# Clears on GpSimd moved behind the x copies, first x tiles loaded from two queues, and some priorities of the instruction planner shifted, in a fused attention and token-mixing kernel

## The chip, the cores and the metric

The kernel runs on one core of one Trainium2 chip. The metric is the device time of one execution in microseconds (us). A profiled execution also has a span, from the first to the last instruction; here it is about 1.8 us shorter than the time. PE is TensorE's matmul unit, DVE is VectorE, ACT is ScalarE, POOL is GpSimd and SP is SyncE, which issues most of the DMA transfers.

Runs of this kernel fall into groups. Below, a "long run" is one more than 1.2 us above the fastest run of the same kernel, and the others are "short runs". Both kinds count as fast runs in the ratios, since the slow state begins at 1.5% above the fastest run; two long runs lie beyond that and are left out of the ratios (188.61 of before and 186.18 of short_close).

## The reference, cut to what matters

```python
x = A_x                                            # (1, 2048, 448) bf16
g = sigmoid((x * gate_w).sum(-1))
# A: 4 segments of 512 tokens, 16 heads of 28: causal softmax inside a segment,
#    plus a linear-attention memory of the segments before, mixed by sigmoid(beta), then @ wo
# B: h = layernorm(x); u = gelu(einsum('bsd,sf->bdf', h, w1) + b1)   # over tokens
#    y = einsum('bdf,fs->bds', u, w2) + b2, transposed back
return g * A(x) + (1 - g) * B(x)
```

## The kernel before

The program is a list of operations with the data they read and write. A planner simulates the five engines and takes, on each engine, the ready operation of the lowest priority number; each engine's instructions are then emitted in that order with semaphores. So a priority or a cost decides the final order.

The loads at the start (SP issues twelve, ACT five):

```python
load_x("SP", 0, 2)                       # x tiles 0 and 1, 224 KB
load_w(wk_nat, WK, R_wk, "wk", P_wk)     # SP: rows 0-255, rows 256-383; ACT: the last 64 rows
load_x("SP", 2, 2)
load_w(wq_nat, WQ, R_wq, "wq", P_wq)     # SP, and the last 64 rows from ACT
load_w(lambda: wvx, WV, R_wv, "wv")      # the same
op("ACT", ... gstage[0:3, :] ...)        # gate weights, two small loads
op("ACT", ... gstage[3:4, :] ...)
# [cut] x tiles 4-15 on SP, beta and the biases
```

The clears on POOL, free to start at once:

```python
op("POOL", lambda e: e.memset(vaug...[:, :, DH:32], 0.0), writes=R_v, name="v0", ...)
op("POOL", lambda e: e.memset(vaug...[:, :, DH : DH + 1], 1.0), reads=R_v, writes=R_v, name="v1", ...)
op("POOL", lambda e: e.memset(wo_sb[:], 0.0), writes=R_wo, name="wo0", ..., rel=8000.0)
op("POOL", lambda e: e.memset(maskg[:], 0.0), writes=[R_maskg], name="maskg0", ..., rel=8000.0)
```

The spread of WK into padded form on DVE, in three pieces as they arrive, which PE's first K projection needs:

```python
for k, (c0, c1) in enumerate(((0, 2), (2, 3), (3, 4))):
    op("DVE", lambda e, c0=c0, c1=c1: e.tensor_copy(wk_pad...[:, c0:c1, :, 0:DH]..., wk_nat()[:, c0:c1, :]...),
       reads=[R_wk[k]] + ..., writes=[R_wkp[k]], name=f"padk{k}", ...)
```

The end: every engine's list is emitted, and SP then waits until each output has landed.

```python
sch.plan()
totals = sch.finalize()
# [cut]
def emit(e, eng=eng):
    sch.emit_engine(e, eng, sems)
    if eng == "SP":
        for sp2 in sorted(sch.out_spaces):      # 17 outputs
            e.wait_ge(sems[sp2], totals[sp2])
```

## Time and profile before

| | before |
|---|---|
| three runs known at the prediction | 185.57, 186.44, 187.23 us (median 186.44) |
| span of the profiled run | 183.5 us (its time: 185.29) |
| PE busy | 96% of the span |
| PE's first K projection | 6.89 us |
| last output operation on DVE starts | 181.01 us |

The first projection and the last DVE operation cut the span into three parts: a start that waits for data (6.89), a long stretch in which PE is the bound (174.12), and a close of 2.5 us. The prediction shows the lines of the first two parts. It does not look at the close.

### The profile page before, as it was taken

How to read it: one execution, taken by the hardware profiler on the slowest of the kernel's cores; microseconds unless marked ns; L12 is line 12 of the kernel's file. 1: busy time of each engine (PE TensorE's matmuls, PEld its weight loads, DVE VectorE, ACT ScalarE, POOL GpSimd, SP SyncE). 2: the span in 40 equal slices, each digit the busy share in tenths (PEclk: the TensorE clock that was granted, in tenths of full speed). 3: DMA queues.
4: the chain of work that ended last, by engine and by line, in shares of the span. 5: the costliest groups of instructions: out<-in, count | busy, mean ns of one | idle time of the engine just before them, and what ended most of it. 6: DMA issues, size and time to landing. Idle time of an engine off the chain costs nothing.

```text
span 183.5 us, 3421 instructions
## 1 busy us (share of the span) xinstructions
PE 176.2 (96%) x1335; PEld 84.3 (46%) x1349; DVE 156.1 (85%) x307; ACT 130.9 (71%) x162; POOL 75.6 (41%) x108
## 2 busy tenths in 40 slices
PE   8599998999999999999999998999999999999994
PEld 3464433444445444444444453545445444445563
DVE  3799999879799999769898999998999989977122
ACT  1497879779999999998989997501799787600500
POOL 8500197143641715446292734512228537552000
PEclk9999999999999999999999999999999999999999
DMA  6998999005958271001446560276601702753001
GB/s 158 317 293 238 276 168 263 21 0 166 224 131 216 41 202 30 0 4 30 126 103 188 50 194 4 54 211 161 189 11 30 212 4 60 215 175 103 27 25 50
DMA packets 46427, 22.80 MB, mean 124 GB/s; under 512 B 11980, under 2 KB 46412, under 8 KB 46412
## 3 DMA queue, kind: packets, MB, share of 16 engines
q1 hardware_dynamic: 46164, 22.42, 48.2%
q8 instruction: 10, 0.16, 0.4%
q10 hardware_dynamic: 248, 0.17, 0.4%
q14 instruction: 5, 0.04, 0.1%
HBM read 18.13 MB, written 1.84 MB: 109 GB/s over the span
## 4 chain that ended last, share of the span: by engine, by line
PE 79%; DVE 10%; ACT 4%; POOL 3%; DMA 2%; issue 1%
PE t L950 24%; PE t L978 23%; PE t L634 10%; PE t L843 6%; PE t L880 6%; PE t L930 5%; PE t L691 3%; ACT t L852 2%; DMA t<-in_A_wk_dram 2%; PE t L726 2%; POOL t L798 2%; DVE t L567 1%; DVE t L788 1%; DVE t L804 1%; DVE t L940 1%; DVE t L704 1%
## 5 line engine op out<-in xcount | busy, mean ns | idle before, releaser
L852 ACT ACTIVATE t<-t 128x2048 bf16<-128x2048 f32 x40 | 75.3, 1883 | 9.8 <-PE t L843 9.7
L855 POOL TENSOR_SCALAR_AFFINE_SELECT t<-t 128x512 bf16<-128x512 bf16 x64 | 49.2, 769 | 52.6 <-ACT t L852 45.6
L950 PE MATMUL t<-t 128*128 128x448 bf16 x224 | 46.4, 353 | 0.3
L978 PE MATMUL t<-t 128*128 128x448 bf16 (+1 forms) x238 | 45.6, 342 | 0.2
L634 PE MATMUL t<-t 128*128 128x512 bf16 (+1 forms) x138 | 29.6, 355 | 2.2 <-DVE t L567 1.9
L978 PEld LDWEIGHTS t<-t 128*128 128x128 bf16 x238 | 22.4, 98 | 19.5 <-issue 1.8
L950 PEld LDWEIGHTS t<-t 128*128 128x128 bf16 x224 | 20.4, 98 | 21.5 <-issue 3.3
L910 POOL TENSOR_TENSOR t<-t 128x448 bf16<-128x448 f32 x12 | 15.3, 1272 | 24.4 <-DVE t L908 23.9
L634 PEld LDWEIGHTS t<-t 128*128 128x128 bf16 x144 | 13.3, 98 | 14.9 <-DVE t L567 2.4
L983 DVE SCALAR_TENSOR_TENSOR t<-t 128x448 bf16<-128x448 f32 (+1 forms) x17 | 11.1, 650 | 10.3 <-PE t L978 8.2
L843 PE MATMUL t<-t 28*128 28x512 bf16 (+3 forms) x256 | 15.8, 301 | 0.7 <-ACT t L705 0.4
L936 ACT ACTIVATE t<-t 128x448 bf16<-128x448 f32 x8 | 5.8, 725 | 11.9 <-PE t L930 11.7
L930 PE MATMUL t<-t 128*128 128x448 bf16 x64 | 13.8, 353 | 0.1
L691 PE MATMUL t<-t 128*128 128x449 bf16 x64 | 13.6, 353 | 0.0
L654 ACT ACTIVATE t<-t 128x512 bf16<-128x512 bf16 x12 | 7.5, 629 | 8.1 <-DMA t<-t 8.1
L896 DVE STREAM_TRANSPOSE t<-t 128x512 f32<-128x512 f32 x16 | 11.3, 704 | 1.6 <-PE t L880 1.5
L647 ACT ACTIVATE t<-t 128x512 bf16<-128x512 f32 (+1 forms) x16 | 8.1, 516 | 6.2 <-PE t L634 5.9
L916 DVE STREAM_TRANSPOSE t<-t 128x512 bf16<-128x512 bf16 x16 | 11.2, 699 | 0.7 <-POOL t L910 0.7
L880 PE MATMUL t<-t 128*32 128x512 bf16 (+3 forms) x256 | 11.6, 302 | 0.0
L967 DVE SCALAR_TENSOR_TENSOR t<-t 128x448 bf16<-128x448 f32 x14 | 10.7, 777 | 0.6 <-ACT t L965 0.5
L962 DVE SCALAR_TENSOR_TENSOR t<-t 128x448 f32<-128x448 f32 x14 | 9.7, 702 | 1.2 <-ACT t L957 1.1
L843 PEld LDWEIGHTS t<-t 28*128 28x128 bf16 x256 | 4.5, 92 | 13.1 <-ACT t L852 6.7
(89 smaller groups left out, 213.1 us busy)
## 6 DMA issues: line engine op xcount, KB each, us to landing
t<-in_B_w_dram SPq DMA_DIRECT2D x7, 1024.0 KB, 6.3
t<-in_B_w_dram SPq DMA_DIRECT2D x8, 896.0 KB, 5.2
out_dram<-t SPq DMA_DIRECT2D x15, 112.0 KB, 2.4
t<-in_A_x_dram SPq DMA_DIRECT2D x3, 448.0 KB, 6.7
t<-in_A_x_dram SPq DMA_DIRECT2D x2, 224.0 KB, 3.8
t<-in_A_wo_dram SPq DMA_DIRECT2D x4, 98.0 KB
t<-in_A_wq_dram SPq DMA_DIRECT2D x1, 336.0 KB, 4.9
t<-in_A_wv_dram SPq DMA_DIRECT2D x1, 336.0 KB, 5.2
```

The costliest lines, as they stand in the source:

```text
L634: last = e.matmul(bank(b)[:, 0:n], w_pad[0:CK, c, hg * 128 : hg * 128 + 128], xT[0:CK, c, tc * 512 + t0 : tc * 512 + t0 + n], start=(c == ...
L691: last = e.matmul(bank(b)[:, 0 : D + 1], xT[0:CK, c, t * 128 : t * 128 + 128], wvx[0:CK, c, 0 : D + 1], start=(c == 0), stop=(c == NCT - 1 ...
L843: last = e.matmul(bank(hl)[:, c0 : c0 + w], kT[r, hg, s * 512 + j * 128 : s * 512 + j * 128 + 128], qT[r, hg, s * 512 + 128 * j : s * 512 ...
L852: op("ACT", lambda e: e.activation(pslot(g), ps[:, 0:4, :], ACT.Exp, scale=SCALE), reads=R_bank[0:4], writes=[g.res], take=g, name=f"exp{p ...
L855: op("POOL", lambda e, c0=c0: e.affine_select(pslot(g)[:, :, c0 : c0 + 128], pslot(g)[:, :, c0 : c0 + 128], pattern=[[0, 4], [1, 128]], co ...
L880: last = e.matmul(bank(cb)[32 * hl : 32 * hl + 32, 128 * j : 512], vaug[:, 4 * s + j, 32 * h : 32 * h + 32], pslot(P_fill[u // 2][f])[:, h ...
L896: dv(lambda e: e.transpose(t2[:, 0, :], bank(cb)[:, 0:512]), [bres(cb)], [R_tt[tb][0]], "ta", 630, use=(cb,))
L910: op("POOL", lambda e: e.tensor_tensor(o3, n3[0], n3[1], op=ALU.add), reads=R_tt[tb], writes=[R_ob[tb]], name=f"o{u}", cost=1280, port=Tru ...
L916: dv(lambda e: e.transpose(oT[:, hg, s * 512 : s * 512 + 512], o), [R_ob[tb]], [R_qT[hg][s]], "ot", 635)
L930: last = e.matmul(bank(b)[:, 0:D], oT[:, hg, T * 128 : T * 128 + 128], wo_sb[:, hg, :], start=(hg == 0), stop=(hg == NHG - 1), skip_group_ ...
L950: op("PE", lambda e, st=st: e.matmul(bank(b)[:, 0:D], w1c[:, st, f2 * 128 : f2 * 128 + 128], xh[:, st, :], start=(st == 0), stop=(st == NT ...
L978: op("PE", lambda e, ft=ft: e.matmul(bank(b)[:, 0 : c1 - c0], w2c[:, ft, t2_ * 128 : t2_ * 128 + 128], uT[:, ft, c0:c1], start=(ft == 0), ...
```

## The change

The intent: POOL should not hold DVE up while DVE prepares the first projection (a copy of 448 columns took 1.47 us beside a clear and 0.26 later); the first x tiles should come from two queues; ACT should issue fewer loads (its five issues lasted until 3.65 us) and be free sooner; and a search with the planner gave 16 groups of operations other priorities. `COLD` is the planner's own estimate, in ns, of how long PE runs slowly at the start (by the clock record of the traces until 4.0 us before and 6.2 after), and it was changed too.

```diff
-COLD = 5000.0
+COLD = 3200.0
@@ plan
+        for o in self.ops:
+            o.prio = (o.prio[0] + shifts.get(o.name.split("-")[0], 0.0), o.idx)
+SHIFTS = (
+    ("mq3_3", -41.28), ("phk2_1", 0.29), ("phq2_2", 1.15), ("prk0_0", 0.51), ("prk0_1", 3.71), ("prk2_1", 10.16),
+    ("prk2_3", -7.78), ("prq2_3", -0.46), ("prt14", -56.47), ("prt3", 39.99), ("prt8", 6.09), ("prt9", -12.18),
+    ("pv0", 6.49), ("pv5", 23.25), ("sc2_1", -46.8), ("tm8", -43.02),
+)
@@ loads
-        op("ACT", lambda e: e.dma_start(dst()[64:128, 3, 0:D], src[384:448]), ...
+        op("SP" if take is not P_wk else "ACT", lambda e: e.dma_start(dst()[64:128, 3, 0:D], src[384:448]), ...
-    load_x("SP", 0, 2)
+    load_x("SP", 0, 1)
+    load_x("ACT", 1, 1)
-    op("ACT", lambda e: e.dma_start(gstage[0:3, :], ...
+    op("SP", lambda e: e.dma_start(gstage[0:3, :], ...
-    op("ACT", lambda e: e.dma_start(gstage[3:4, :], ...
+    op("SP", lambda e: e.dma_start(gstage[3:4, :], ...
@@ clears, now emitted after the x transposes
-    op("POOL", ... vaug ... 0.0), writes=R_v, name="v0", ...)
+        op("POOL", ... vaug ... 0.0), reads=[R_xT0[1][0]], writes=R_v, name="v0", ...)
-    op("POOL", ... wo_sb[:], 0.0), writes=R_wo, name="wo0", ..., rel=8000.0)
+        op("POOL", ... wo_sb[:], 0.0), reads=[R_xT0[1][0]], writes=R_wo, name="wo0", ...)
[the same for maskg0; renamed groups and one cost for the planner cut]
-    sch.plan()
+    sch.plan(SHIFTS)
```

`R_xT0[1][0]` is the second transposed block of x that DVE copies.

More of the change, by code (lines that the diff above doesn't have):

```diff
@@ L147, in op, with plan @@
         return o
-    def plan(self):
+    def plan(self, shifts=()):
         import bisect
+        shifts = dict(shifts)
+        for o in self.ops:
+            o.prio = (o.prio[0] + shifts.get(o.name.split("-")[0], 0.0), o.idx)
         succ = [[] for _ in self.ops]
@@ L450, in load_x @@
         op(eng, lambda e: e.dma_start(xh[:, t0 : t0 + n, :], xv[:, t0 : t0 + n, :]),
-           writes=R_x[t0 : t0 + n], name=f"ldx{t0}", dma=True, cost=500 if n == 2 else 1300, nbytes=n * 128 * 896)
+           writes=R_x[t0 : t0 + n], name=f"ldx{t0}", dma=True, cost=500 if n < 4 else 1300, nbytes=n * 128 * 896)
     def load_w(dst, src, r, name, take=None):
@@ L458, in load_w @@
                take=None if k else take)
-        op("ACT", lambda e: e.dma_start(dst()[64:128, 3, 0:D], src[384:448]), writes=[r[-1]], name="ld" + name + "b",
+        op("SP" if take is not P_wk else "ACT", lambda e: e.dma_start(dst()[64:128, 3, 0:D], src[384:448]),
+           writes=[r[-1]], name="ld" + name + "b",
            dma=True, cost=500, nbytes=57344)
@@ L472, in build_kernel @@
     load_w(lambda: wvx, WV, R_wv, "wv")
-    op("ACT", lambda e: e.dma_start(gstage[0:3, :], GW[0:384].rearrange("(c p) -> c p", p=128)),
+    op("SP", lambda e: e.dma_start(gstage[0:3, :], GW[0:384].rearrange("(c p) -> c p", p=128)),
        writes=[R_gst[0]], name="ldgw", dma=True, cost=500, nbytes=2000)
-    op("ACT", lambda e: e.dma_start(gstage[3:4, :], GW[320:448].rearrange("(c p) -> c p", p=128)),
+    op("SP", lambda e: e.dma_start(gstage[3:4, :], GW[320:448].rearrange("(c p) -> c p", p=128)),
        writes=[R_gst[1]], name="ldgwb", dma=True, cost=500, nbytes=2000)
@@ L529, in build_kernel @@
        name="wqp0", cost=pool_cost(256))
-    op("POOL", lambda e: e.memset(vaug.rearrange("p t (h c) -> p (t h) c", c=32)[:, :, DH:32], 0.0), writes=R_v,
-       name="v0", cost=pool_cost(1024))
-    op("POOL", lambda e: e.memset(vaug.rearrange("p t (h c) -> p (t h) c", c=32)[:, :, DH : DH + 1], 1.0),
-       reads=R_v, writes=R_v, name="v1", cost=pool_cost(256))
-    op("POOL", lambda e: e.memset(wo_sb[:], 0.0), writes=R_wo, name="wo0", cost=pool_cost(1792), rel=8000.0)
-    op("POOL", lambda e: e.memset(mhalf[:], -0.5), writes=[R_mhalf], name="mhalf", cost=200)
-    op("POOL", lambda e: e.memset(maskg[:], 0.0), writes=[R_maskg], name="maskg0", cost=pool_cost(512), rel=8000.0)
     def load_wo():
@@ L542, in load_wo, with pool_clears @@
                reads=[R_wv[0]], writes=[R_wo[hl]], name=f"ldwo{hl}", dma=True, cost=500, nbytes=126000)
+    def pool_clears():
+        op("POOL", lambda e: e.memset(vaug.rearrange("p t (h c) -> p (t h) c", c=32)[:, :, DH:32], 0.0),
+           reads=[R_xT0[1][0]], writes=R_v,
+           name="v0", cost=pool_cost(1024))
+        op("POOL", lambda e: e.memset(vaug.rearrange("p t (h c) -> p (t h) c", c=32)[:, :, DH : DH + 1], 1.0),
+           reads=R_v, writes=R_v, name="v1", cost=pool_cost(256))
+        op("POOL", lambda e: e.memset(wo_sb[:], 0.0), reads=[R_xT0[1][0]], writes=R_wo, name="wo0", cost=pool_cost(1792))
+        op("POOL", lambda e: e.memset(mhalf[:], -0.5), writes=[R_mhalf], name="mhalf", cost=200)
+        op("POOL", lambda e: e.memset(maskg[:], 0.0), reads=[R_xT0[1][0]], writes=[R_maskg], name="maskg0", cost=pool_cost(512))
     rr = [0]
@@ L628, in transposes_1, with proj_d @@
                alt=("ACT", lambda e, io=io: e.activation(*io(), ACT.Copy), act_cost(1024)))
-    def proj_d(w_pad, R_w, hg, tc, b, t0=0, n=512):
+    def proj_d(name, w_pad, R_w, hg, tc, b, t0=0, n=512):
         def fn(e):
@@ L639, in proj_d @@
         need = R_xT[tc] if tc else [r for h in range(2) if t0 < 256 * h + 256 and t0 + n > 256 * h for r in R_xT0[h]]
-        op("PE", fn, reads=need + R_w, writes=[bres(b)], **btake(b), name=f"prd{tc}_{hg}", mode="f",
+        op("PE", fn, reads=need + R_w, writes=[bres(b)], **btake(b), name=f"{name}{tc}_{hg}" + ("h" if t0 else ""), mode="f",
            cost=pe_cost(n, n, n, n), prio=PRJ[tc] + (0.01 if t0 else 0))
@@ L645, in do_k @@
         ks = kT[:, hg, tc * 512 + t0 : tc * 512 + t0 + n]
-        proj_d(wk_pad, R_wkp, hg, tc, b, t0, n)
+        proj_d("prk", wk_pad, R_wkp, hg, tc, b, t0, n)
         op("ACT", lambda e: e.activation(ks, bank(b)[:, 0:n], ACT.Copy),
@@ L667, in do_q @@
         qs = qT[:, hg, tc * 512 : tc * 512 + 512]
-        proj_d(wq_pad, R_wqp, hg, tc, b)
+        proj_d("prq", wq_pad, R_wqp, hg, tc, b)
         op("DVE", lambda e: e.tensor_copy(qs, bank(b)[:, 0:512]), **buse(b), reads=[bres(b)], writes=[R_qT[hg][tc]],
@@ L951, in mm1 @@
                                                start=(st == 0), stop=(st == NT - 1), skip_group_check=True),
-               reads=[R_slot[fb % NSL], R_x[st]], writes=[bres(b)], take=b if st == 0 else None, name=f"u{ft}_{st}", mode="f", cost=pe_cost(448),
+               reads=[R_slot[fb % NSL], R_x[st]], writes=[bres(b)], take=b if st == 0 else None, name=f"u{ft}-{st}", mode="f", cost=pe_cost(448),
                prio=P_M1 + ft)
@@ L981, in mm2 @@
                reads=[R_slot[r]] + (R_uT if ft == 0 else [R_uT[ft]]), writes=[bres(b)],
-               take=b if ft == 0 else None, name=f"y{T}_{ft}", mode="f", cost=pe_cost(c1 - c0), prio=P_M2 + T)
+               take=b if ft == 0 else None, name=f"y{T}-{ft}", mode="f", cost=pe_cost(c1 - c0), prio=P_M2 + T)
         op("DVE", lambda e: e.scalar_tensor_tensor(outst[:, p, c0:c1], bank(b)[:, 0 : c1 - c0], omg[:, T : T + 1],
@@ L996, in build_kernel @@
     transposes_0(1)
+    pool_clears()
     for t0 in (0, 256):
```

## The prediction

> **What bounds the kernel now.** I read the page first (engines, then the slices), then the chain that ended last, then the timeline of PE, DVE and POOL over the first 35 us, then the DMA issues. From the page, PE's row and two groups:
>
> ```profile
> PE 176.2 (96%) x1335; PEld 84.3 (46%) x1349; DVE 156.1 (85%) x307; ACT 130.9 (71%) x162; POOL 75.6 (41%) x108
> ...
> L852 ACT ACTIVATE t<-t 128x2048 bf16<-128x2048 f32 x40 | 75.3, 1883 | 9.8 <-PE t L843 9.7
> ...
> L634 PE MATMUL t<-t 128*128 128x512 bf16 (+1 forms) x138 | 29.6, 355 | 2.2 <-DVE t L567 1.9
> ```
>
> PE is the bound, and L634 (the K and Q projections) is the only matmul group with a large wait before it. The start of the chain says what that wait is:
>
> ```profile
> 0.81 3.32 DMA t<-in_A_wk_dram
> 4.15 2.17 DVE t L567 x2
> 6.32 0.33 DVE t L599
> 6.65 0.20 DVE t L567
> 6.89 0.61 PE t L634 x4
> ```
>
> The columns are start, length, work. DVE needs 2.5 us after the arrival of WK to spread it into padded form (L567) and to copy the first transposed x (L599); until 6.89 PE has only warm-up and one set of transposes. The timeline shows why the first spread is slow: one copy of 448 columns takes 1.47 us while POOL clears `wo_sb` (L534), and the same shape later takes 0.26.
>
> ```profile
> 3.59 1.90 POOL L534 MEMSET t<- 128x1792 bf16 x1
> 4.15 1.47 DVE L567 COPY t<-t 128x448 bf16<-128x448 bf16 x1 [1.98 <-DMA t<-in_A_wk_dram]
> 6.57 0.26 DVE L567 COPY t<-t 128x448 bf16<-128x448 bf16 x1
> ```
>
> How full is PE afterwards? Busy time can't tell, since matmuls overlap, so I count work by the distance between groups: 20 MLP matmuls of 448 columns go from 40.98 to 44.87, 0.1945 us each; 12 of 512 columns take 2.70 (0.225 each); a fill of scores (L843) 0.33, a PV (L880) 0.66. From the first projection on there are 562 matmuls of 448 or 449 columns (109.3 us), 112 of 512 in projections and 12 in the memory read (27.9), 32 of 256 (3.7), 28 of 224 (2.6), 40 fills (13.2), 16 PVs (10.6), 3 memory updates (2.9), 24 transposes and two small ones (1.6): 171.8 us. PE runs from 6.89 to 181.01, that is 174.1. So after its first projection PE stands still for only about 2.4 us in all. I find 2.0 of it: the last V tiles before the MLP (4 matmuls in 1.18 instead of 0.78; 12 in 2.88 instead of 2.33, both around fills that wait for ACT), the first MLP tile (14 in 3.14 instead of 2.72), and 0.6 at 111.8 to 113.2. The rest of the kernel is packed.
>
> The first MLP tile waits for the layer norm, a long DVE and POOL chain:
>
> ```profile
> 24.09 2.92 POOL t L798
> 27.01 0.60 POOL t L855
> 27.62 0.07 issue
> 27.68 0.62 POOL t L799
> 28.30 0.07 issue
> 28.38 0.23 POOL t L801
> 28.63 1.39 DVE t L804 x2
> ```
>
> L798 to L801 make the coefficients; a causal mask (L855) sits between them for 0.6 us, and L804 applies them tile by tile.
>
> [...] the copy that came at 4.15 ended at 5.62, just after L534's end at 5.49, 1.2 us later than its own 0.26 would give. [...] an issue costs 0.43 to 0.64 us on SP, 0.53 to 0.71 on ACT for the larger ones, and the DMA engines are already at share 0.9 to 1.2 from 2 us on. [...] here the 176.2 us busy include overlap, which is why I counted distances.
>
> **The change part by part.**
>
> *POOL clears behind the x copies.* Four clears (0.95 + 1.21 + 1.90 + 0.65 = 4.7 us) move from 1.8-6.1 to after the second x copy on DVE, near 8. The two L567 copies shrink from 2.17 to about 0.26 + 0.35 (the second is twice as wide), some 1.5 us. But the third copy needs the middle piece of WK, whose DMA is issued at 1.80 and takes 4.6 us: it lands at 6.4, only 0.2 before the copy ran. So with these arrivals PE could start at 6.4 + 0.26 + 0.06 = 6.7, a gain of 0.2. Most of the 1.5 us turns into a DMA wait.
>
> *Loads.* x's first two tiles come from SP and ACT (115 KB each); ACT then issues only WK's last piece, second instead of first; WQ's and WV's last pieces go to SP behind. Until the middle piece of WK has landed some 115 KB fewer compete (the two 57 KB pieces are later), at about 290 KB/us some 0.4 us: estimate 6.0. Against it, WK's last piece is now ACT's second issue at about 1.35, and ACT's second issue took 4.3 us before: 5.6, and DVE's order still asks for it first. Then 5.6 + 0.26 + 0.35 + 0.40 + 0.26 + 0.06 = 6.9 if all runs after it, 6.3 if it comes at 5.0. I take PE's first projection at 6.5: gain 0.4. SP's later x loads are issued about 2.1 us later (four more issues), at 6.1 instead of 4.0; WV, ahead of them in the queue, lands at 8.7, so the DMA engines should hardly run dry.
>
> *Order on PE.* Before, four fills stood among the projections, and PE reached the MLP at 31.16. Now all 32 projections for tokens 0 to 1023 and nine V tiles come first, then 2 MLP matmuls, a fill, 11 more, a fill, 3 more. Work before the MLP: the 24.3 us from 6.89 to 31.16, less its four fills (1.3), plus a V tile (0.8), less the 0.95 of waits on ACT: 22.8, so PE comes at 6.5 + 22.8 = 29.3. DVE's statistics contain one V eviction more (0.6) and one K eviction less (0.4): last aggregate near 23.2. Without the mask the POOL part is 4.75 instead of 5.35: coefficients at 28.0, then 16 applications in a row at 0.32 each (7 took 2.22 before), done at 33.1. PE needs 16 x 0.1945 + 2 x 0.33 = 3.8 us for the same stretch, 29.3 to 33.1. It just fits, with perhaps 0.3 of waiting. So the 1.4 us of waits in this region fall to about 0.7, counting V evictions that crowd on ACT (0.54 + 0.17 a tile against PE's 0.78).
>
> *The other shifts.* They redistribute the last 1 us of waits, and nothing more is there to win: I take 0.2.
>
> Sum: 0.4 + 0.7 + 0.2 = 1.3 us off 186.44: 185.1.
>
> **Rivals.** *The full 1.5 us is won at the start* and all waits go: 186.44 - 1.5 - 2.4 = 182.5. For it: the contention is real. Against: WK's 6.4 arrival and the layer norm's own length; PE merely arriving earlier would wait there. *The contention moves to WQ*: its spread (L574, 0.62 at 8.77) now meets the clears at about 8; it would be held by up to 0.95 (first clear), at worst 2.9 (two). Q's first matmul comes at about 10.2, so one clear hides, two cost about 1 us and delay the layer norm as well: 186 to 187. *ACT becomes the bound*: exponentials start some 7 us later and the mid part is ACT's fullest (slices 9 or 8 from 41 to 118 us); but ACT has idle stretches after (8.1 us before 126, 10.9 before 171) and the new order on PE moves fills into them. If it is wrong PE waits 1 to 3 us: 186 to 188.
>
> **Range and chances.** A kernel with no waits left would stand at 186.44 - 0.4 - 2.4 = 183.6, so that is about my lower end; the upper end is the change winning nothing. Over 2% faster needs 182.7, below that floor unless WK comes over a microsecond earlier: 0.05. Over 2% slower needs 3.7 us of new waits: 0.02.
>
> **What would show it.** Right: L567's first two copies near 0.26 and 0.35, a DMA wait before one of them; first L634 at 6.2 to 6.8; POOL's L798 followed directly by L799; PE groups 29 to 34 us short of waits; the same work of 171.8 us after. Wrong: first L634 at 5.5 or below; L574 stretched over 1.5 us; fills waiting for ACT in mid-kernel; PE waits of over 2 us after 35 us.

## The result, and the profile after

| | before | after |
|---|---|---|
| runs | 185.57, 185.57, 185.64, 186.44, 187.23, 187.23 | 183.87, 184.04, 184.14, 184.15, 184.23, 184.60 |
| median | 186.04 us | 184.14 us |
| span of the profiled run | 183.5 us | 182.1 us |

The ratio is 0.9887 (95% interval 0.9846 to 0.9927), which is "same" at 2%. A ratio is the mean time of one kernel's fast runs over that of the other's of the same rounds, so it is not quite the ratio of the medians. Two of the six runs of before are long runs and none of after's; the short runs of before have a median of 185.56 over all 143 runs of it that were made in this study, those of after 184.15 over its twelve: 1.41 us less.

Two lines of the page of after:

```profile
PE 178.0 (98%) x1349; PEld 85.1 (47%) x1349; DVE 154.0 (85%) x307; ACT 132.7 (73%) x162; POOL 73.6 (40%) x108
...
L649 PE MATMUL t<-t 128*128 128x512 bf16 (+1 forms) x144 | 30.8, 358 | 0.0
```

L649 is the group of K and Q projections that was L634 before (the new lines shift the numbers by 13 to 15). Its wait of 2.2 us is gone, and PE is busy for 98% of the span instead of 96%. The timeline of after over the start (columns: start, length, engine and line, operation, count, and in brackets how long the engine had been idle and what ended it):

```profile
4.48 0.58 DVE L582 COPY t<-t 128x448 bf16<-128x448 bf16 x2 [2.31 <-DMA t<-in_A_wk_dram]
4.98 0.41 DVE L614 COPY t<-t 128x512 bf16<-128x512 bf16 x1
5.31 0.27 DVE L582 COPY t<-t 128x448 bf16<-128x448 bf16 x1
5.64 0.87 PE L649 MATMUL t<-t 128*128 128x256 bf16 x4
...
7.77 1.14 DVE L589 COPY t<-t 128x1792 bf16<-128x1792 bf16 x1
```

L582 is the spread of WK (L567 before): the first two now take 0.58 together instead of 2.17. DVE waits for WK's data, not for POOL. The third copy runs at 5.31 instead of 6.57, because its piece of WK comes sooner; the rows of DMA issues (the last columns are KB and us from issue to landing), before and after, with the issue at 1.81 and 1.73:

```profile
t<-in_A_wk_dram SPq DMA_DIRECT2D x1, 112.0 KB, 4.6
...
t<-in_A_wk_dram SPq DMA_DIRECT2D x1, 112.0 KB, 3.5
```

L589 is the spread of WQ, which now meets the clears: 1.14 us instead of 0.62. Not all of the earlier start is a gain: by the trace's clock record PE is granted its full rate only at 6.2 us here (4.0 before), so it takes 0.71 us over the first four matmuls, up to the next group, instead of 0.45.

The chain of after through the layer norm's coefficients (start, length, work), and PE's timeline round the first MLP tile:

```profile
23.91 3.25 POOL t L813
27.16 0.08 issue
27.24 0.21 POOL t L814
```

```profile
28.75 0.54 PE L965 MATMUL t<-t 128*128 128x448 bf16 x2
29.50 0.39 PE L858 MATMUL t<-t 28*128 28x512 bf16 x4 [0.21 <-ACT t L720]
29.83 2.44 PE L965 MATMUL t<-t 128*128 128x448 bf16 x11
32.20 0.40 PE L858 MATMUL t<-t 28*128 28x384 bf16 x8
32.53 1.10 PE L965 MATMUL t<-t 128*128 128x448 bf16 x3
33.48 1.03 PE L649 MATMUL t<-t 128*128 128x512 bf16 x4
```

The mask between L813 and L814 is gone. The applications (L819) run in a row from 27.78 to 33.22. PE reaches its MLP at 28.75. The tile's 16 matmuls and two fills take 4.73 us against 3.77 of work (16 at 0.1945 and two at 0.33), so PE still waits for about 1.0 us there.

The last is the close. The last row of each timeline is the last DVE operation, before and after (spans 183.5 and 182.1):

```profile
181.01 0.45 DVE L983 SCALAR_TENSOR_TENSOR t<-t 128x224 bf16<-128x224 f32 x1 [0.89 <-PE t L978]
...
179.18 0.45 DVE L998 SCALAR_TENSOR_TENSOR t<-t 128x224 bf16<-128x224 f32 x1 [0.89 <-PE t L993]
```

From the start of this operation to the end of the span it takes 2.5 us before and 2.9 after. With it the account of the two profiled runs is: start 6.89 to 5.64, -1.25; stretch from there to the last DVE operation 174.12 to 173.54, -0.58; close +0.4. The sum, -1.4, is the difference of the spans. So there are two gains and a loss, and the change is made of three kinds of edit; the experiments assign them.

### The profile page after: what moved, and what is told of

It is laid out like the page before. It is cut to its first block, busy times and chain, and to the rows that moved or that the text cites. A ratio compares the mean times of both kernels' runs of the same rounds, so it can differ in the third digit from the quotient of the medians.

```text
span 182.1 us, 3439 instructions
## 1 busy us (share of the span) xinstructions
PE 178.0 (98%) x1349; PEld 85.1 (47%) x1349; DVE 154.0 (85%) x307; ACT 132.7 (73%) x162; POOL 73.6 (40%) x108
## 4 chain that ended last, share of the span: by engine, by line
PE 89%; DVE 6%; POOL 2%; issue 0%
PE t L993 24%; PE t L965 23%; PE t L649 13%; PE t L945 7%; PE t L858 7%; PE t L895 6%; PE t L706 3%; DVE t L819 3%; PE t L573 2%; POOL t L813 2%; PE t L881 2%; PE t L741 1%; DVE t L803 1%; PE t L601 1%; PE t L630 1%; DVE t L794 0%
## 5 line engine op out<-in xcount | busy, mean ns | idle before, releaser
L870 POOL TENSOR_SCALAR_AFFINE_SELECT t<-t 128x512 bf16<-128x512 bf16 x64 | 48.6, 760 | 59.2 <-ACT t L867 56.5
L993 PE MATMUL t<-t 128*128 128x448 bf16 (+1 forms) x238 | 46.4, 342 | 0.0
L649 PE MATMUL t<-t 128*128 128x512 bf16 (+1 forms) x144 | 30.8, 358 | 0.0
L925 POOL TENSOR_TENSOR t<-t 128x448 bf16<-128x448 f32 x12 | 14.1, 1171 | 20.6 <-DVE t L923 20.6
L649 PEld LDWEIGHTS t<-t 128*128 128x128 bf16 x144 | 13.4, 99 | 13.2 <-DVE t L582 0.9
L951 ACT ACTIVATE t<-t 128x448 bf16<-128x448 f32 x9 | 6.5, 734 | 15.7 <-PE t L945 15.6
L673 DVE SCALAR_TENSOR_TENSOR t<-t 128x512 bf16<-128x512 bf16 x12 | 10.5, 883 | 0.0
L969 ACT ACTIVATE t<-t 128x448 f32<-128x448 f32 x14 | 9.0, 644 | 1.2 <-PE t L965 1.2
```

What stands on the lines that cost most here:

```text
L649: last = e.matmul(bank(b)[:, 0:n], w_pad[0:CK, c, hg * 128 : hg * 128 + 128], xT[0:CK, c, tc * 512 + t0 : tc * 512 + t0 + n], start=(c == ...
L870: op("POOL", lambda e, c0=c0: e.affine_select(pslot(g)[:, :, c0 : c0 + 128], pslot(g)[:, :, c0 : c0 + 128], pattern=[[0, 4], [1, 128]], co ...
L925: op("POOL", lambda e: e.tensor_tensor(o3, n3[0], n3[1], op=ALU.add), reads=R_tt[tb], writes=[R_ob[tb]], name=f"o{u}", cost=1280, port=Tru ...
L993: op("PE", lambda e, ft=ft: e.matmul(bank(b)[:, 0 : c1 - c0], w2c[:, ft, t2_ * 128 : t2_ * 128 + 128], uT[:, ft, c0:c1], start=(ft == 0), ...
```

## The experiments

Twelve kernels ran. Most keep the order of all operations fixed, so that an edit of the loads can't also change the plan: the planner's result was recorded as a list, and a replay takes the engine and buffer of each operation from it.

```diff
-    sch.plan(SHIFTS)
+    sch.replay(LINE)      # LINE: the recorded order of before or of after
```

The traces bear this out: after_again shows the instructions of after with the same waits on every engine, except for some matmul records that are missing, and clears_alone those of before, except for the moved clears. Numbers of the first projection, the stretch and the close are from one profiled run each; "short" is the median of the short runs. All verdicts are "same" at 2%, except short_close: "unclear", its interval reaching below 0.98.

| kernel | order | loads | clears | median us | short | long runs | ratio (95%) | first proj. | close |
|---|---|---|---|---|---|---|---|---|---|
| clears_alone | old | old | moved | 185.68 | 185.59 | 4 of 22 | 0.9988 (0.9961-1.0014) | 6.62 | 2.07 |
| loads_alone | old | new | early | 185.96 | 185.94 | 5 of 22 | 1.0025 (1.0002-1.0048) | 6.89 | 2.48 |
| clears_loads | old | new | moved | 185.70 | 185.67 | 2 of 14 | 0.9995 (0.9964-1.0026) | 6.05 | 2.48 |
| order_alone | new | old | early | 184.34 | 184.33 | 3 of 11 | 0.9941 (0.9907-0.9974) | 6.93 | 2.08 |
| order_loads | new | new | early | 184.71 | 184.68 | 5 of 22 | 0.9956 (0.9933-0.9980) | 6.88 | 2.47 |
| order_clears | new | old | moved | 184.36 | 184.36 | 0 of 7 | 0.9919 (0.9888-0.9950) | 6.59 | 2.08 |
| after_again | new | new | moved | 184.13 | 184.13 | 0 of 6 | 0.9911 (0.9878-0.9943) | 5.96 | 2.47 |
| clears_after_wq | new | new | moved on | 184.35 | 184.30 | 2 of 10 | 0.9920 (0.9889-0.9952) | 5.96 | 2.49 |
| x_split | new | x only | moved | 184.15 | 184.15 | 0 of 6 | 0.9895 (0.9845-0.9944) | 6.91 | 2.06 |
| pieces_moved | new | pieces only | moved | 184.24 | 184.22 | 1 of 18 | 0.9906 (0.9881-0.9932) | 6.95 | 2.49 |
| longer_sp | new | old | moved | 184.37 | 184.30 | 5 of 22 | 0.9917 (0.9891-0.9943) | 6.47 | 2.31 |
| short_close | new | new | moved | 183.89 | 183.79 | 1 of 6 | 0.9857 (0.9794-0.9920) | 5.85 | 2.06 |

The close is here counted from the end of the last DVE operation to the end of the span. The four calls to the chip held the kernels in this order: the first three and order_alone; order_loads, after_again, order_clears, clears_after_wq; x_split, pieces_moved, longer_sp; short_close. The short runs of before in them had medians of 185.44, 185.55, 185.58 and 185.59.

### clears_alone

```diff
@@ before, order of before
+ clears: reads=[R_xT0[1][0]]
```

> The order of every engine is that of the kernel before; only POOL's four clears wait for the second x copy. My theory ([...] the arrival of WK's middle piece at 6.4 us): first K projection at 6.6 to 6.75 instead of 6.89, and the time at most 0.3 us (0.2%) shorter. Rival [...]: first K projection near 5.6, over 1 us (0.6%) shorter.

Measured: the first projection at 6.62, the time as before. The timeline of clears_alone:

```profile
6.28 0.28 DVE L712 COPY t<-t 128x448 bf16<-128x448 bf16 x1 [0.99 <-DMA t<-in_A_wk_dram]
...
8.49 1.14 DVE L719 COPY t<-t 128x1792 bf16<-128x1792 bf16 x1
...
31.20 3.22 PE L1095 MATMUL t<-t 128*128 128x448 bf16 x14
```

The wait for POOL has become a wait for DMA, as predicted, and 0.27 us are won at the start. But the MLP (L1095) starts at 31.20 against 31.16 before. DVE works without a pause from here to the layer norm's coefficients. They come as late as before, because the WQ spread (L719) is 0.5 us longer. In the old order this earlier start of PE is eaten before 31 us.

### loads_alone

```diff
@@ before, order of before
+ loads: x tiles 0, 1 from SP and ACT; last pieces of WQ and WV and the gate weights on SP
```

> Order of the kernel before, clears as before, only the loads changed. My theory: WK's middle piece lands at 5.2 as in the changed kernel, but the first WK spread is still held by the clear of wo_sb to about 5.6, so the first K projection comes at 6.7 to 6.9 and the time is at most 0.3 us shorter. Rival (the loads alone held the start): first K projection before 6.0, over 0.8 us shorter.

The start does not move while the clears stand in DVE's way (the first two copies take 1.91 us together). The time is 0.25% longer, just outside the interval's edge at 1. The close accounts for it: 2.48 instead of 2.07.

### clears_loads

```diff
@@ before, order of before
+ both edits
```

> Order of the kernel before with both the moved clears and the changed loads. My theory: the two together bring the first K projection to 5.6, 1.2 us earlier, far more than the sum of the two alone; and since PE is packed afterwards, 0.8 to 1.2 us of it (0.4 to 0.6%) arrive at the end. Rival (the layer norm, which follows DVE, sets the end of the first stage): the waits before the first MLP tile grow by what the start gained, and the time falls by less than 0.4 us.

My theory of 0.8 to 1.2 us fell; the rival's time came. The first projection came at 6.05, and the time is that of before. The profiled run was a long one (187.81), so the rival's mechanism can be seen only in clears_alone. Part of the reason is the close: against loads_alone, which has the same long close and starts at 6.89, the short runs are 0.27 us shorter, for a start 0.84 earlier.

### order_alone

```diff
@@ before's loads and clears
+ sch.replay(LINE)   # order of after
```

> Loads and clears as before, order of every engine that of the changed kernel. My theory: the first K projection stays at 6.9, the waits of PE between the V tiles and the first MLP tile fall from 1.3 us to about 0.7, and the time is 0.4 to 0.9 us (0.2 to 0.5%) shorter. Rival (the order is fitted to the early start and is worth nothing without it): same time as before within 0.2%.

The order alone is worth more than the 0.4 to 0.9 I expected: 185.44 to 184.33 in short runs of the same call, 1.11 us, with the same start. From clears_alone to order_clears it is 1.23, and from loads_alone to order_loads 1.26, though these pairs stand in two calls. The profiled run was a long one, so the waits of my theory can't be read from it; and what made the planner's order (`COLD`, the 16 shifts or the moved operations) was not separated.

### order_loads

```diff
@@ order of after
+ loads of after, clears of before
```

> The changed kernel with POOL's clears put back to the start. My theory: DVE's WK spreads are held by the clears again, first K projection at 6.3 to 6.9, runs in the upper cluster again, lowest time about that of the new order alone (184.3), mean 0.3 to 0.6% longer than the changed kernel. Rival (the moved clears are not needed once the loads are early): within 0.1% of the changed kernel.

The first projection and the long runs came as expected. The lowest time, 184.64, is 0.35 above the 184.3 expected, and so are the short runs above order_alone's: this is the longer close (0.39). The profile fell on a long run, and shows what a long run is. PE's timeline of order_loads, from the first projection:

```profile
6.88 1.04 PE L780 MATMUL t<-t 128*128 128x256 bf16 x4 [2.21 <-DVE t L713]
7.70 1.06 PE L732 MATMUL t<-t 128*128 128x128 bf16 x8
8.56 4.93 PE L780 MATMUL t<-t 128*128 128x256 bf16 x27
```

And the same rows in order_clears, a short run:

```profile
6.59 0.61 PE L778 MATMUL t<-t 128*128 128x256 bf16 x4 [0.79 <-DVE t L711]
7.34 0.62 PE L730 MATMUL t<-t 128*128 128x128 bf16 x8
7.80 4.14 PE L778 MATMUL t<-t 128*128 128x256 bf16 x27
```

The same matmuls take 1.04 or 0.61, 1.06 or 0.62, 4.93 or 4.14: 0.43 + 0.44 + 0.79 = 1.7 us, the distance between the groups of runs. In the long run PE worked at its full rate at 4.07 (two matmuls of 512 columns in 0.60 us), stood idle for 2.21 us and then worked at half of it until 10.3. The view by stretches of order_loads has the granted clock in the column before the last two (stretch, length, PE busy with count, clock, DMA share, GB/s):

```profile
3.50:6.80 3.30, 1.17 (x12) 1.00 0.99 274
6.90:10.10 3.20, 3.20 (x20) 0.50 1.00 314
10.40:14.00 3.60, 3.55 (x33) 1.00 1.14 237
```

The long run of pieces_moved looks the same, after 2.11 us of idle time. That of order_alone does not: its clock record begins at 10.2 us, and before PE went idle for 1.14 us its eight transposes took 1.03 us and its two matmuls of 512 columns 1.06 (0.61 and 0.60 in order_loads). So PE had not yet reached its full rate then.

### after_again

```diff
@@ order of after, loads and clears of after: the kernel after
```

> The changed kernel once more (built from its recorded order, instruction for instruction the same), as the yardstick of this set: 1.0 to 1.2% shorter than before. About 3 in 10 runs of the kernel before lie 1.7 us above the others. My theory: these are runs in which PE, idle for 1.9 us ahead of the first K projection, falls back to half its clock and does the first projections cold; the changed kernel leaves no such gap, so none or few of its runs (under 1 in 10) lie over 1.2 us above its lowest. Rival (the upper cluster has nothing to do with the gap): again about 3 in 10.

It repeats after: 184.13, first projection at 5.96, no long run in six. The half clock of the theory is what order_loads' long run shows (0.50, after 2.21 us of idle time); no long run of before was profiled. The ratio, 0.9% shorter than before, is a little under the 1.0 to 1.2% expected.

### order_clears

```diff
@@ order of after, loads of before
+ clears: reads=[R_xT0[1][0]]
```

> The changed kernel with the old loads. My theory: WK's middle piece lands at 6.2 to 6.4 again, first K projection at 6.5 to 6.7, lowest time within 0.2 us of the new order alone (184.3), and upper-cluster runs again. Rival (the moved clears alone do it): within 0.1% of the changed kernel.

The start is as expected, but the long runs I expected did not come (0 of 7), the lowest time, 183.74, is 0.5 below order_alone's and not within 0.2 of it, and the median is only 0.2 us above after's. In the new order the earlier start is handed on as far as the MLP: from the first projection to the first MLP matmul it is 23.13 us here and 23.11 in after, against 24.27 before and 24.58 in clears_alone.

The first MLP matmuls start at 29.72 here and at 28.75 in after: 0.97 earlier, for a start that is 0.95 earlier. So the new loads do bring almost 1 us in after's profiled run, but part of it is lost again, and the close is 0.4 of that. The rest is within what the runs of one kernel differ by (183.74 to 184.67 here). Among the kernels of the new order with the short close, short runs have 184.33, 184.36 and 184.15 with starts of 6.93, 6.59 and 6.91 (order_alone, order_clears, x_split) and 183.79 with a start of 5.85 (short_close): 0.4 to 0.6 us of time for 0.7 to 1.1 us of start, from few runs in several calls.

### clears_after_wq

```diff
@@ after
-           reads=[R_xT0[1][0]], writes=R_v,
+           reads=R_wqp, writes=R_v,        # behind the spread of WQ
[the same for wo0 and maskg0]
```

> The changed kernel with the clears waiting for the WQ spread on DVE instead of the second x copy. In the changed kernel that spread took 1.14 us instead of 0.62, behind POOL's first clear. My theory: it takes 0.62 again, statistics and layer-norm coefficients come 0.3 to 0.5 us earlier, PE's waits at the first MLP tile shrink by as much, and the time falls by 0.2 to 0.4 us. Rival (PE arrives there no earlier, V evictions on ACT set it): same time within 0.1 us.

The WQ spread takes 0.63 again and the statistics start at 8.41 instead of 8.89, but DVE then waits 0.31 at 17.23 for a transpose on PE, and the coefficients come only 0.1 us earlier. No time is won: the 0.5 us that the spread takes longer in after costs next to nothing.

### What made WK's piece early: x_split and pieces_moved

```diff
@@ x_split: order and clears of after, loads of before
-    load_x("SP", 0, 2)
+    load_x("SP", 0, 1)
+    load_x("ACT", 1, 1)
@@ pieces_moved: order and clears of after, loads of before
+    last pieces of WQ and WV and the gate weights: op("SP", ...) instead of op("ACT", ...)
```

> The new order and the moved clears, with only one edit of the loads: the first two x tiles are loaded as two pieces by SP and ACT; the last pieces of WQ and WV and the gate weights stay on ACT, so SP issues twelve loads at the start as before, not sixteen. My theory: WK's middle piece comes early because SP has 112 KB less ahead of it, so it lands at 5.2 to 5.7 us and the first K projection starts at 5.6 to 6.1 as in the kernel after; and the longer close (from the end of the last VectorE operation to the end of the span 2.45 us in every kernel with sixteen loads on SP, 2.05 with twelve) goes with SP's number of instructions, so it is 2.0 to 2.1 here. The time is then 0.3 to 0.5 us below the kernel after: 183.6 to 183.9. Rival 1: the early WK piece needs the last pieces off ACT: first projection at 6.4 to 6.7, time as order_clears, 184.2 to 184.5. Rival 2: the long close comes with the split x load itself: close 2.45, time 184.0 to 184.3.

> The new order and the moved clears, with only the other edit of the loads: the last pieces of WQ and WV and the gate weights go from ACT to SP, the first two x tiles stay one load of SP. My theory: nothing early is gained (first K projection at 6.4 to 6.7 as in order_clears) and SP's four more instructions make the close long (2.45 us): 0.4 us longer than order_clears, 184.6 to 185.0. Rival 1 (the pieces off ACT make room for WK's piece): first projection at 5.6 to 6.1. Rival 2 (the long close comes with the split x load): close 2.05, time as order_clears, 184.2 to 184.5.

My theory that the split of x alone does it fell: x_split's first projection came at 6.91, later than even the rival had it. Its close is short, as I expected. In pieces_moved the first projection was at 6.95, later than the 6.4 to 6.7 expected, and the close long, as I expected. Its time missed the 184.6 to 185.0: its profiled run was a long one, and its short runs (184.22) are shorter than a start at 6.95 with a long close would give, so that single look may not stand for them. What stands: all five kernels that have both load edits and the moved clears had the first projection between 5.64 and 6.05, and all five with moved clears and at most one of the two between 6.47 and 6.95. The landings of WK's middle piece, issued between 1.71 and 1.82 everywhere, say the same without the clears in the way: 6.1 to 6.4 us in the five traces with the old loads, 4.9 to 5.9 in the seven with both edits, loads_alone (5.87) and order_loads (5.69) among them, and 6.55 and 6.59 in x_split and pieces_moved. Why the two are needed together is open.

### The close: longer_sp and short_close

The views leave branches out, but the trace has them. The last wait of SP ends when the last output has landed, 1.58 to 1.61 us after its issue began in all kernels. SP's closing branch then starts 0.06 us after it in the kernels with twelve loads on SP (78 records of SP), and 0.45 to 0.47 us after it in those with sixteen (82 records). So a longer SP program, or the loads themselves, could be the cause.

```diff
@@ longer_sp: order_clears, and on SP ahead of the closing waits
+                    first = sorted(sch.out_spaces)[0]
+                    for _ in range(4):
+                        e.wait_ge(sems[first], totals[first])     # long met
```

> order_clears (the new order and the moved clears, the loads of before) with four more waits in SP's program at its end, each on a semaphore that is long met by then, beside the wait for the last output. Nothing is loaded differently. My theory: the 0.4 us more at the close of the kernels with sixteen loads on SP is the closing branch of SP, which starts 0.09 us after the last wait in the kernels with the old loads and 0.49 us after it in those with the new ones, because SP's program is four instructions longer [...]. So here the branch starts 0.45 to 0.53 us after the last wait, the close is 2.4 to 2.5 us, and the time is 0.3 to 0.5 us above order_clears: 184.65 to 184.9. Rival: the close belongs to the loads (their queue, their transfers): branch 0.09 us after the last wait, close 2.0 to 2.1, time 184.2 to 184.5.

Half of this missed. The four waits became two instructions (80 records), the branch started 0.04 us after the last wait, and the close was 2.31, between the two. The stall was still there, two records later: the last record of SP came 0.46 us after the one before it, against 0.16 in order_clears. So the stall stands ahead of SP's 80th record here, and in after too, where the 80th of 82 is the branch. This fits a stall at a fixed place of SP's program, which the branch reaches with four more instructions. The time, 184.37, could not tell 0.24 us. Then the opposite, on the kernel after:

```diff
@@ short_close: the kernel after
-                if eng == "SP":
-                    for sp2 in sorted(sch.out_spaces):
-                        e.wait_ge(sems[sp2], totals[sp2])
+                waits = sorted(sch.out_spaces)
+                for sp2 in {"POOL": waits[:8], "SP": waits[8:]}.get(eng, []):
+                    e.wait_ge(sems[sp2], totals[sp2])
```

> The kernel after, with eight of the seventeen waits for outputs, which SP makes at its end, made by POOL at its end instead: SP's program is again as long as in order_clears, and everything else, the loads and the order too, is that of the kernel after. My theory (the close is long when SP's closing instructions fall behind a fixed place of its program, which four more instructions reach, and which the two more of longer_sp reached two instructions later): the last branch of SP starts within 0.1 us of the last wait, the close is 2.0 to 2.1 us instead of 2.45 to 2.49, the first K projection stays at 5.6 to 6.1, and the median is 183.6 to 183.9, 0.25 to 0.5 us below the kernel after (184.14), the fastest of all kernels here. Rival (the long close comes with the loads after all, or the wait moves to POOL's end): close 2.3 or more, median 184.0 to 184.3.

All of it was met. SP has 78 records, the branch starts 0.065 us after the last wait, and the timeline of short_close (span 181.8) ends like this:

```profile
179.32 0.45 DVE L998 SCALAR_TENSOR_TENSOR t<-t 128x224 bf16<-128x224 f32 x1 [0.89 <-PE t L993]
```

That is 2.5 us from the last DVE operation to the end again, with all of after's loads in place. The short runs have a median of 183.79 against after's 184.15, in another call; this is the fastest of all kernels here, though the intervals of the two ratios overlap and only the trace separates them. I looked for a transfer of instructions in the stall. The traces record the DMA packets that carry instructions (queues of kind "instruction" on the pages, fifteen packets within each span), and the view of the DMA in after from 181.2 to 181.8, which covers the stall, has none, nor any other packet:

```profile
DMA packets 0, 0.00 MB, mean 0 GB/s; under 512 B 0, under 2 KB 0, under 8 KB 0
```

In all seven kernels with this stall the last packet of instructions before the branch is 7 to 10 us old, and the next starts 0.21 to 0.25 us after the end of the span (0.62 in longer_sp, 1.1 to 1.4 in the six others). So no transfer of instructions is shown in the stall. What the stall is stays open; that a few instructions on SP decide it is shown.

### Long runs

Over all calls, kernels with the clears early had 60 long runs in 198 (before itself 47 in 143), those with the clears moved 15 in 117. The share is more than halved, and this adds to the difference of means and medians: it is why the ratio says 1.1% where short runs say 0.8%. Moving the clears does not end them: clears_alone and longer_sp still had 9 in 44. The record has a mean granted clock for 73 of the long runs and 236 short ones. It is 0.989 to 0.991 in 44 of the long ones, 36 of them with the clears early, and below 0.998 in no short one. The profiled runs of order_loads and pieces_moved, in which PE fell back to half its rate, have 0.990, which speaks for the same in the rest of these. In the other 29 it is 0.998 to 1.0; the profiled run of order_alone, whose clock record begins at 10.2 us, is one of them. What makes one run of a program long and the next one short is not settled. x_split had an idle time of 1.65 us before the first projection in a short run, order_alone 1.14 in a long one, and short_close, with its early start, had a long run in six.

## Why the prediction was right or wrong

The time, 184.14, lies inside the range and 1.0 us below the predicted 185.1. The gain, 1.3, is near the 1.41 between short runs, but this is partly luck: the start and the order brought more than was allowed for and the close, which was left out, took 0.4 back.

- **The base, "1.3 us off 186.44", was the step that failed most.** (174.1 less 171.8 is 2.3, not 2.4; nothing hangs on it.) Of the three runs then known, 186.44 lay between the two groups: the short runs' median is 185.56. The gain of 1.3 taken from that gives 184.26. The profile that was read had a time of 185.29 and showed which group it belonged to.
- **"PE could start at 6.4 + 0.26 + 0.06 = 6.7, a gain of 0.2"** from the clears was right: 6.62 in clears_alone. The hold-up beside POOL's clears was there and went away (the first copy took 1.47 us before and 0.28 in clears_alone), and most of its 1.5 us became a DMA wait. What it brought to the time in the old order was nothing.
- **"I take PE's first projection at 6.5: gain 0.4" was mis-sized.** WK's middle piece landed at 5.2 and 5.6 in after's two profiles, not at the estimated 6.0; WK's last piece came at 4.4 to 4.5, below the 5.0 to 5.6 allowed for. The first projection came at 5.64 and 5.96, a gain of 0.9 to 1.25. The estimate counted bytes ahead at one rate. But pieces_moved has the same loads ahead of this piece as after, on one queue instead of two, and the copy of it started at 6.62 against 5.31 (in one look each).
- **"It just fits, with perhaps 0.3 of waiting" and "to about 0.7"** had the arrivals right and the waits too small: PE came at 28.75 (29.3 predicted) and the applications ran from 27.78 to 33.22 (28.0 to 33.1), but PE waited 1.0 us in the tile, not 0.3. The V tiles before it lost next to nothing (24 matmuls in 4.72 us). So the 1.4 us of waits fell to 1.0, a gain of 0.4 where 0.7 was taken. The removed mask did what was said.
- **"The other shifts ... I take 0.2"** was too little. The order in all was worth 1.1 to 1.3 us in short runs, against 0.7 + 0.2; less the 0.4 above, 0.7 to 0.9 of it came from elsewhere. One visible part is the 0.6 us at 111.8 to 113.2, which is gone.
- **The close is a term that the sum did not have:** 0.4 us lost, by four more instructions on SP.
- **The rivals.** Contention did move to the WQ spread, by 0.52 us (1.14 us against 0.62), within the "up to 0.95"; clears_after_wq gained nothing by removing it. ACT did not become the bound. The full gain at the start nearly came, but PE did not lose all its waits.
- **Signs.** Seen as listed: the two short copies with a DMA wait, L798 followed directly by L799 (now L813 and L814), the spread of WQ below 1.5. Missed: a first projection of 6.2 to 6.8, and PE short of waits from 29 to 34 us.

The effect of POOL's clears on DVE is seen both ways: L567's two copies fell from 2.17 to 0.58, and the WQ spread rose from 0.62 to 1.14 beside the moved clears. For the loads, counting bytes alone was my estimate; those two looks, copies at 6.62 and 5.31 with the same bytes ahead, speak for the mix of queues having a part, which no run here explains.

## What to carry to other kernels

A delay removed at the start reaches the end only if the next chain that PE depends on moves with it: an earlier start was worth little in the old order (0.27 us for 0.84), and in the new one 0.95 us of it made the MLP start 0.97 us earlier, of which about half reached the time. Take a base from the group of runs that the profile belongs to. And look at the last two microseconds: instructions added to an engine that does little can cost there, and moving a few waits to an idle engine can win that back (four more instructions on SP cost 0.4 us here, and eight waits moved to POOL took it back).
